# Attention into a feed-forward layer on one core: batch 2's queries and keys by transposed loads instead of TensorE transposes, with a new order of the front

## The chip, the cores and the metric

The kernel runs on one core of a Trainium2 chip. The metric is the device time of one execution in microseconds (us); several executions of the same program are timed and their median is given. One execution is also taken by the hardware profiler; the times inside it are counted from the start of its span.

## The reference

Eight batches of twelve heads, 448 positions, 64 values per head. Attention with a softmax that has one more term in its sum, then a feed-forward layer with a squared relu over all 3,584 tokens. The kernel is given float32 arrays and gives a float32 array.

```python
q, k, v: (8, 12, 448, 64)         # * 0.1
scores = q @ k.T / sqrt(64)
m = max(scores);  e = exp(scores - m)
attn = e / (sum(e) + exp(-m) + 1e-09)
x = (attn @ v).transpose(0, 2, 1, 3).reshape(3584, 768)
h = x @ w_in                      # (768, 2048)
out = (relu(h) ** 2) @ w_out      # (2048, 768)
```

## The kernel before, in words

All matmuls are in float16. For each batch the kernel needs the queries and keys with the 64 values of a head on the partitions (the tile `qk`, two buffers), the values in natural layout (`vn`, two buffers), and then the attention output `xt` as the left side of the first layer.

Queries and keys come to that layout in one of two ways.

- For a batch in `ON_PE` (0, 1 and 2 before), `load_quad` loads a quad (four heads) of q and of k in natural layout into a tile `nn` (line 117, POOL's DMA queue, cast to float16 on the way), `transpose_one` turns it by 14 TensorE transposes for q and 14 for k (line 207), and `transposed_copy` copies the result from PSUM to `qk` (line 215 on ACT, line 217 on VectorE).
- For any other batch, `stage` writes q and k of the batch as float16 to a DRAM buffer (line 155, POOL's queue), `transposed_load` reads it three times with the transposing DMA on SP's queue (line 166): the queries, the keys, and the keys shifted by one row ("planes" 0, 1, 2). Since heads then lie in rows of two positions, the last 64 keys of each head are gathered by `tail_keys`: two POOL copies for each key plane (line 188). The values of such a batch come by four DMAs (line 111), those of a batch in `ON_PE` by one for each quad or one for the batch.

The scores of one chunk of 64 keys of a quad are four matmuls of 64x448 for a batch in `ON_PE` and eight of 64x224 for any other (`quad_scores`, lines 415 and 429); ACT takes the exponential of the chunk (line 254). A score buffer holds one chunk; there are two (`s_psum`). Each quad has seven chunks. Then VectorE adds the chunks (lines 441 to 447), TensorE sums over the partitions (`S`), ACT takes a logarithm (line 463, `Z`) and a negative exponential (line 466, `M`), and VectorE multiplies the values' product by it into `xt` (line 487, `X`).

The first layer of a batch is 16 tiles of six matmuls (`j`, three steps of two each), each followed by a relu (`k`, ACT line 503 or VectorE line 505) and a square (`l`, line 509). The second layer is 56 half tiles of 128 tokens by 384 columns (`o`), 16 blocks of four quarter-array matmuls each, put out by two operations (`O`, `Q`) into one of four output buffers `ot` and stored by DMAs on SP's queue (line 549). First-layer tiles, value products and second-layer tiles share a ring of four PSUM buffers.

The order of all work is written out by hand. `ORDER` is the front: it does the attention of batches 0 to 3, the first layer of batches 0 and 1, and the first 14 half tiles of the second layer. Each word is a step, such as `s48` (scores, exponentials are `e48`), `j11,4,6` or `o1,8,10`; `d` steps are entries of the list `LOADS`. Scores 24 to 44 are batch 1's, 45 to 65 batch 2's, 66 to 86 batch 3's. Behind the front come two runs of `CYCLE` (periods for batches 4 and 6) and a tail of plain first- and second-layer tiles. A step issues its instructions to the engines' queues in this order, and each engine works its own queue off in order, waiting where a semaphore makes it wait. POOL's queue holds its DMA issues and the key copies, SP's queue the transposed loads and the stores. POOL's DMA issues wait, by their semaphores, for the landing of the one issued eight before.

## Time and profile before

| | |
|---|---|
| median of 3 runs | 392.39 us (392.35 to 392.91) |
| profiled execution | 393.06 us |
| its span, first to last instruction | 391.3 us |
| granted TensorE clock | 1.00 |
| busy: TensorE, VectorE, ACT, POOL | 383.2, 251.9, 228.5, 62.2 us |
| POOL's DMA queue (q0) | 22.62 MB, 37.4% of 16 engines' span |
| SP's DMA queue (q1; ACT's first loads are q10) | 21.59 MB, 28.1% |
| first period's first scores start | 135.0 us |

In the profile PE is TensorE's matmuls, DVE is VectorE, L93 is line 93 of the kernel, which is the helper that records nearly every matmul. A row of the timeline gives the start, the length, the engine, the line, the operation with its output and inputs, their shapes and how many instructions were merged into the row. Matmul ends are modelled and overlap, so work on TensorE is best read from one start to the next.

### The profile page before, as it was taken

Reading aid. Unit: us, or ns where it says so; the run is one execution under the profiler, and the core shown is the slowest. Engines: PE = TensorE matmul, PEld = TensorE weight load, DVE = VectorE, ACT = ScalarE, POOL = GpSimd, SP = SyncE. Lnnn points to the kernel's source line nnn. Section 1 sums busy time; section 2 is a strip of 40 time slices with the busy share of each in tenths; the row PEclk is TensorE's granted clock in tenths of the full one; section 3 lists DMA queues with packets and bytes.
Section 4 is the critical chain, followed back from the end, with each engine's and each line's share of the span. In section 5 each row is a group of like instructions: output and inputs, shape, how many; then the busy total and the mean of one; then the engine's idle time right before and its main releaser. Section 6 shows DMA issues by size and latency. Waiting matters only on the chain.

```text
span 391.3 us, 14259 instructions
## 1 busy us (share of the span) xinstructions
PE 383.2 (98%) x6432; PEld 253.7 (65%) x6432; DVE 251.9 (64%) x468; ACT 228.5 (58%) x308; POOL 62.2 (16%) x96
## 2 busy tenths in 40 slices
PE   9789999999999999999999999999999999999997
PEld 5566656565789755667777665667777755556665
DVE  2887995765666766556968757566778788880000
ACT  5999998586689511349988731248988730001221
POOL 8544420025000701300001240310000000000000
PEclk9999999999999999999999999999999999999999
DMA  8999999999939899903129596941112200001132
GB/s 143 203 205 205 202 203 205 182 182 175 215 75 175 158 195 149 160 2 66 44 54 194 145 182 131 151 46 44 52 55 64 64 23 2 0 0 61 62 82 80
DMA packets 75052, 45.34 MB, mean 116 GB/s; under 512 B 47472, under 2 KB 72944, under 8 KB 74992
## 3 DMA queue, kind: packets, MB, share of 16 engines
q0 software_dynamic: 24752, 22.62, 37.4%
q1 hardware_dynamic: 49952, 21.59, 28.1%
q8 instruction: 50, 0.82, 0.9%
q10 hardware_dynamic: 288, 0.23, 0.2%
q14 instruction: 10, 0.08, 0.1%
HBM read 45.69 MB, written 17.93 MB: 163 GB/s over the span
## 4 chain that ended last, share of the span: by engine, by line
PE 86%; ACT 6%; DMA 2%; SPq 2%; DVE 1%; issue 1%; POOL 1%; ACTq 0%; POOLq 0%; DVEq 0%
PE mp L93 77%; PE sp L93 8%; ACT et L254 4%; SPq L166 2%; DMA nn<-in_k_dram 2%; PE mp L207 1%; DMA out_dram<-ot 1%; ACT rcp L372 1%; ACT nn L254 0%; DVE qk L217 0%; ACT rcp L365 0%; ACT ot L575 0%; DVE half L341 0%; ACT rcp L463 0%; DVE half L447 0%
## 5 line engine op out<-in xcount | busy, mean ns | idle before, releaser
L93 PE MATMUL mp<-wout,gs 64*64 64x384 f16 (+2 forms) x2928 | 165.2, 322 | 0.0
L93 PE MATMUL mp<-xt,win 128*64 128x448 f16 (+2 forms) x1188 | 148.3, 347 | 0.1
L93 PEld LDWEIGHTS <-gs 64*64 64x64 f16 (+1 forms) x2928 | 103.1, 106 | 34.5
L93 PEld LDWEIGHTS <-win 128*64 128x64 f16 (+1 forms) x1188 | 83.2, 106 | 63.5 <-issue 4.2
L254 ACT ACTIVATE et<-sp 128x896 f16<-128x896 f32 (+2 forms) x131 | 110.6, 889 | 12.3 <-PE sp L93 11.7
L505 DVE TENSOR_SCALAR rt<-mp 128x448 f16<-128x448 f32 x87 | 54.1, 622 | 17.4 <-PE mp L93 14.5
L509 DVE TENSOR_TENSOR gs<-rt 128x448 f16<-128x448 f16 x128 | 47.8, 390 | 22.1 <-ACT rt L503 20.2
L503 ACT ACTIVATE rt<-mp 128x448 f16<-128x448 f32 x41 | 21.8, 543 | 65.0 <-PE mp L93 55.7
L575 ACT ACTIVATE ot<-mp 128x384 f32<-128x384 f32 (+2 forms) x31 | 14.9, 480 | 71.6 <-PE mp L93 68.8
L93 PE MATMUL sp<-qk 64*64 64x224 f16 (+1 forms) x1056 | 53.7, 274 | 2.1 <-DVE qk L217 0.5
L93 PEld LDWEIGHTS <-qk 64*64 64x64 f16 x1056 | 32.7, 115 | 15.2 <-issue 6.5
L188 POOL COPY flatq<-qk 64x384 f16<-64x384 f16 x20 | 14.8, 739 | 172.7 <-DMA qk<-stage_k 126.0
L254 ACT ACTIVATE nn<-sp 128x896 f16<-128x896 f32 x42 | 37.1, 916 | 4.3 <-PE sp L93 4.2
L487 DVE TENSOR_TENSOR xt<-mp,rcp 128x448 f16<-128x448 f32 x42 | 24.2, 619 | 15.7 <-ACT rcp L466 10.3
L581 DVE SCALAR_TENSOR_TENSOR ot<-mp,ot 128x384 f32<-128x384 f32 x42 | 23.4, 556 | 15.3 <-ACT ot L575 12.4
L93 PEld LDWEIGHTS <-vn 64*64 64x64 f16 x756 | 22.4, 107 | 10.4 <-issue 1.8
L93 PE MATMUL mp<-et,vn 64*64 64x448 f16 (+1 forms) x448 | 24.5, 343 | 0.0
L577 DVE TENSOR_SCALAR ot<-mp 128x384 f32<-128x384 f32 x26 | 14.4, 555 | 14.3 <-PE mp L93 14.2
L463 ACT ACTIVATE rcp<-sp,one_b 128x896 f32<-128x896 f32 x21 | 21.1, 1007 | 2.8 <-PE sp L93 2.7
L466 ACT ACTIVATE rcp<-rcp 128x896 f32<-128x896 f32 x21 | 19.9, 949 | 0.5
L441 DVE TENSOR_TENSOR half<-et 128x1792 f16<-128x1792 f16 x15 | 16.3, 1088 | 4.3 <-ACT et L254 4.2
L443 DVE TENSOR_TENSOR half<-half,et 128x1792 f16<-128x1792 f16 x15 | 16.3, 1086 | 0.3
(59 smaller groups left out, 197.4 us busy)
## 6 DMA issues: line engine op xcount, KB each, us to landing
out_dram<-ot SPq DMA_DIRECT2D x52, 96.0 KB, 2.9
out_dram<-ot SPq DMA_DIRECT2D x19, 192.0 KB, 1.9
win<-in_moe_w_in_dram POOLq DMA_DIRECT2D x8, 384.0 KB, 12.3
wout<-in_moe_w_out_dram POOLq DMA_DIRECT2D x4, 768.0 KB, 14.9
vn<-in_v_dram POOLq DMA_DIRECT2D x10, 288.0 KB, 8.4
stage_q<-in_q_dram POOLq DMA_DIRECT2D x4, 676.0 KB, 13.1
stage_k<-in_k_dram POOLq DMA_DIRECT2D x4, 676.0 KB, 15.9
nn<-in_q_dram POOLq DMA_DIRECT2D x8, 224.0 KB, 8.6
```

Source lines behind the costliest of these rows:

```text
L93: return nc.tensor.matmul(out_, lhsT, rhs, start=start, stop=stop)
L254: nc.scalar.activation(out=out_, in_=in_, func=AF.Exp, scale=scale)
L441: nc.vector.tensor_add(esq[m], a[:, 0:w], a[:, w:2 * w])
L443: nc.vector.tensor_add(esq[m], esq[m], z[:, 0:w])
L463: nc.scalar.activation(out=rcp, in_=zp[:, :, 0:S], func=AF.Ln, bias=one_b)
L466: nc.scalar.activation(out=zqs[m], in_=zqs[m], func=AF.Exp, scale=-1.0)
L487: nc.vector.tensor_mul(xts[b][:, 2 * g + i, :], xqs[m][i][:, 0:S], zqs[m][:, i, :])
L503: nc.scalar.activation(out=rt[:, 0:m], in_=hp[:, 0:m], func=AF.Relu)
L505: nc.vector.tensor_scalar(out=rt[:, 0:m], in0=hp[:, 0:m], scalar1=0.0, scalar2=None, op0=ALU.max)
L509: nc.vector.tensor_mul(gs[:, f0:f0 + per, t0 % RING:t0 % RING + n], r, r)
L575: nc.scalar.activation(out=ot, in_=op[:, 0:w], func=AF.Copy, scale=OUT_SCALE)
L581: nc.vector.scalar_tensor_tensor(out=ot, in0=lo[:, 0:w], scalar=OUT_SCALE, in1=ot, op0=ALU.mult, op1=ALU.add)
```

## The change

Batch 2 leaves `ON_PE`. Its natural loads, transposes and copies go; it is staged, loaded by three transposed loads and gets key copies, like batches 3 and later; its values come by four DMAs. The single steps for the three planes and the two key planes are entries of `LOADS` of their own. The staging of batch 5, which stood in the front (`d31`), is now the step `d7` of the first period. `ORDER` is written anew: batch 0 first, the first layer of batch 0 with the attention of batch 1, then the whole first layer of batch 1 by itself, then the 14 half tiles of the second layer with the attention of batches 2 and 3. In POOL's queue the first two key copies of batch 2 (`d24`) now stand ahead of the second half of `wout` (`d17`, `d18`) and of the staging of batch 3 (`d26`), and the next two (`d25`) ahead of the values of batch 2 (`d20`) and 3 (`d27`). In SP's queue batch 2's three transposed loads (`d22`, `d23`, `d21`) and the first of batch 3 (`d28`) stand ahead of the first stores, the other two of batch 3 (`d30`, `d29`) behind the first and the second pair of stores. The periods and the tail keep their order.

```diff
-    ON_PE = (0, 1, 2)
+    ON_PE = (0, 1)
...
-        x = {(0, 1): (0, 0), (0, 2): (0, 1), (1, 0): (1, 0), (1, 1): (0, 0), (1, 2): (0, 1),
-             (2, 0): (1, 0), (2, 1): (1, 1), (2, 2): (0, 0)}[b, g]
+        x = {(0, 1): (0, 0), (0, 2): (0, 1), (1, 0): (1, 0), (1, 1): (0, 0), (1, 2): (0, 1)}[b, g]
...
-    LOADS = ([lambda b=b, g=g: load_quad(b, g) for b in range(3) for g in range(NQ) if b + g]
+    LOADS = ([lambda b=b, g=g: load_quad(b, g) for b in range(2) for g in range(NQ) if b + g]
              + [lambda b=b, g=g: load_v_quads(b, g, g + 1) for b in range(2) for g in range(NQ)]
-             + [lambda: load_v_quads(2)]
              + [lambda i=i: load_win(i, NW) for i in range(NW)]
-             + [lambda n0=n0, y=y: load_wout(n0, y, 2) for n0 in (0, HALF) for y in range(2)]
-             + [lambda: stage(3), lambda: transposed_loads(3), lambda: tail_keys(3), lambda: load_v_quads(3),
-                lambda: stage(4), lambda: transposed_loads(4), lambda: tail_keys(4), lambda: load_v_quads(4), lambda: stage(5)])
+             + [lambda n0=n0, y=y: load_wout(n0, y, 2) for n0 in (0, HALF) for y in range(2)])
+    for b in (2, 3, 4):
+        LOADS += [lambda b=b: stage(b), lambda b=b: load_v_quads(b)]
+        LOADS += [lambda b=b, i=i: transposed_load(b, i) for i in range(3)]
+        LOADS += [lambda b=b, i=i: tail_keys(b, (i,)) for i in (1, 2)]
...
     ORDER = """
...
+        l8 k2,1 l9 k0,1 l2 j1,0,2 j1,2,4 j13,0,2 j13,2,4 j4,0,2 j4,2,4 j4,4,6 j1,4,6 j14,0,2 j14,2,4 j14,4,6 j13,4,6 k1,1 l0 j15,0,2 k13,0 j15,2,4
+        j15,4,6 l1 j5,0,2 l13 k4,0 d24 d17 d18 d26 k14,1 l4 j5,2,4 j5,4,6 s48 o0,0,2 o0,2,4 k5,1 l14 e48 k15,0 s45 l15 o0,4,6 o0,6,8 o0,8,10 s49 d28
+        o0,10,12 o0,12,14 e45 o0,14,16 s46 e49 e46 s50 O0,0 o1,0,2 Q0 o1,2,4 o1,4,6 o1,6,8 s47 e50 o2,0,2 s55 o2,2,4 o1,8,10 e47 o1,10,12 d25 d20 e55
+        s56 o1,12,14 a3,0 l5 d30 e56 s53 a3,1 o2,4,6 o2,6,8 o1,14,16 e53 s51 O1,1 o2,8,10 s54 o2,10,12 o2,12,14 o2,14,16 e51 j10,0,2 Q1 d29 a3,2
+        j10,2,4 j10,4,6 a3,3 k10,1 j3,0,2 e54 j3,2,4 j3,4,6 O2,0 k3,1 Q2 v3,0 S3 v3,1 v3,2 v3,3 v3,4 Z3 v3,5 v3,6 M3 o5,0,2 s52 e52 o5,2,4 o5,4,6
...
     """
...
-            if t < B and (n != 7 or b > FIRST_PERIOD):
+            if t < B:
```

More of the change, by code (lines that the diff above doesn't have):

```diff
@@ L676 @@
     ORDER = """
-        d0 W8 d8 d1 c1,4,0 c0,0,1 t0,0,0 c1,0,1 t1,0,0 u0,0,0,0 t1,0,4 u1,0,0,0 c0,4,1 u1,0,4,1 t0,0,4 d2 s0 t0,1,0 u0,0,4,1 u0,1,0,0 t1,1,0 u1,1,0,0
-        d10 d9 s1 t0,1,4 e0 t1,1,4 e1 s2 e2 u0,1,4,0 s12 e12 u1,1,4,0 T0,1,0 T0,1,1 U0,1,0,0,4,0 U0,1,1,0,4,0 U0,1,1,4,7,0 U0,1,0,4,7,0 s3 s4 p2 p0 e3
-        b0,0 e4 s6 p1 d18 p3 s5 e6 e5 b0,1 b0,2 T0,2,0 b0,3 y0 T0,2,1 U0,2,0,0,4,0 z0 n0 U0,2,1,0,4,0 b1,0 s8 U0,2,0,4,7,0 U0,2,1,4,7,0 x0 d3 d17 d16
-        b1,1 s9 d15 T1,0,1 e8 e9 U1,0,1,0,7,0 T1,0,0 U1,0,0,0,7,0 b2,0 s11 e11 s10 s13 e10 e13 s14 p8 b2,1 p4 d5 b2,2 p9 s7 e14 p10 b2,3 p11 y2 p5 e7
@@ L681 @@
-        z2 b1,2 p6 s15 b1,3 p7 e15 y1 b3,0 n2 x2 b3,1 z1 s17 e17 b3,2 p12 p13 b3,3 n1 s18 p14 s16 e18 p15 x1 y3 T1,1,0 U1,1,0,0,7,0 e16 b4,0 z3 b4,1
-        s19 e19 i0,6 n3 r0,6,0 s20 e20 s21 i0,7 s22 x3 b4,2 e21 p16 b4,3 e22 b5,0 r0,7,0 p17 p18 p19 d4 b5,1 g0,6 y4 z4 n4 s23 T1,1,1 e23 d13 s27 b5,2
-        x4 i0,4 s28 p20 p21 g0,7 b5,3 e27 p22 p23 y5 U1,1,1,0,7,0 e28 z5 r0,4,0 n5 x5 s26 s29 e26 j20,0,2 j23,0,2 j23,2,4 j20,2,4 j20,4,6 e29 j23,4,6
-        s25 k23,1 s24 g0,4 e25 e24 k20,0 P0 i1,7 j19,0,2 l23 a0,0 s32 e32 a0,1 s36 d6 j19,2,4 e36 j16,0,2 l20 j19,4,6 j17,0,2 s34 s33 k19,1 r1,7,0
@@ L685 @@
-        j17,2,4 j16,2,4 a0,2 l19 e34 j17,4,6 e33 j16,4,6 g1,7 s30 d11 k16,1 s31 e30 k17,0 T2,0,0 T1,2,0 T2,0,1 T1,2,1 l16 s35 e31 U2,0,0,0,7,0
-        U1,2,0,0,7,0 s37 U2,0,1,0,7,1 e35 j18,0,2 j18,2,4 e37 j18,4,6 a0,3 i1,6 d19 S0 U1,2,1,0,7,0 v0,0 a1,0 v0,1 Z0 v0,2 l17 v0,3 v0,4 v0,5 k18,0 d7
-        d12 v0,6 s40 s43 M0 r1,6,0 j27,0,2 a1,1 e43 j22,0,2 j22,2,4 j27,2,4 X0 e40 j27,4,6 l18 j22,4,6 g1,6 a1,2 s39 k27,1 s38 e39 a1,3 d20 T2,2,0 e38
-        k22,0 T2,2,1 T2,1,1 T2,1,0 s41 U2,2,1,0,7,1 U2,2,0,0,7,0 s42 j26,0,2 l27 e41 j21,0,2 j26,2,4 j26,4,6 l22 S1 U2,1,0,0,7,0 e42 U2,1,1,0,7,0 Z1
@@ L689 @@
-        v1,0 v1,1 v1,2 v1,3 v1,4 d23 v1,5 k26,1 v1,6 a2,0 a2,1 a2,2 s44 s47 M1 l26 e44 j21,2,4 d22 j21,4,6 i1,4 X1 a2,3 k21,1 v2,0 v2,1 v2,2 r1,4,0 S2
-        e47 v2,3 Z2 v2,4 v2,5 l21 v2,6 M2 o0,0,4 s46 o0,4,8 d14 s50 e46 e50 o0,8,12 X2 o0,12,16 s51 g1,4 s48 O0,1 Q0 j15,0,2 j0,0,2 j15,2,4 j4,0,2
-        j15,4,6 j4,2,4 j4,4,6 j0,2,4 e51 e48 j0,4,6 s45 k15,1 l15 o2,0,4 s49 e45 e49 o2,4,8 s52 d21 o2,8,12 a3,0 e52 o2,12,16 k4,1 k0,0 s53 a3,1 s55
-        d24 j10,0,2 O2,1 j1,0,2 Q2 j10,2,4 j1,2,4 j10,4,6 l0 j14,0,2 l4 j1,4,6 j11,0,2 e55 k10,0 j14,2,4 a3,2 j11,2,4 k1,1 j8,0,2 l10 j14,4,6 j11,4,6
@@ L693 @@
-        k11,1 j9,0,2 a3,3 j8,2,4 j9,2,4 e53 l1 j8,4,6 j9,4,6 k14,0 s57 l14 e57 l11 S3 Z3 v3,0 d25 v3,1 v3,2 v3,3 k9,0 k8,0 v3,4 v3,5 v3,6 M3 o1,0,4
-        s54 o1,4,8 X3 s56 o1,8,12 o1,12,16 e54 a4,0 O1,0 s63 e56 o5,0,4 s58 o5,4,8 Q1 e63 a4,1 a4,2 s65 e58 a4,3 o5,8,12 e65 s60 o5,12,16 e60 O5,1 s59
-        v4,0 v4,1 Q5 v4,2 v4,3 l9 S4 v4,4 e59 Z4 M4 v4,5 v4,6 o4,0,4 o4,4,8 s61 o4,8,12 o4,12,16 e61 s64 O4,1 X4 s62 j2,0,2 l8 Q4 j2,2,4 j2,4,6 j7,0,2
-        k2,1 j5,0,2 e62 j7,2,4 j7,4,6 k7,0 l7 d27 j12,0,2 j6,0,2 e64 a5,0 j12,2,4 j5,2,4 l2 j5,4,6 k5,1 j6,2,4 j6,4,6 j12,4,6 a5,1 j13,0,2 j13,2,4
@@ L697 @@
-        j13,4,6 l5 a5,2 j3,0,2 j3,2,4 j3,4,6 k12,0 a5,3 s69 l12 k6,1 o3,0,4 l6 k13,1 k3,1 l3 S5 l13 o3,4,8 o3,8,12 o3,12,16 O3,0 Q3 e69 s70 Z5 s71 d26
-        M5 v5,0 v5,1 v5,2 v5,3 e70 e71 v5,4 v5,5 v5,6 o9,0,2 o9,2,4 X5 o9,4,6 o9,6,8 s66 o9,8,10 s68 o9,10,12 o9,12,14 o9,14,16 e66 O9,0 o6,0,2 e68
-        s67 s72 o6,2,4 o6,4,6 o6,6,8 e67 o6,8,10 Q9 a6,0 a6,1 e72 a6,2 s73 o8,0,2 o6,10,12 o6,12,14 o8,2,4 o6,14,16 s75 e73 O6,0 o8,4,6 o8,6,8 e75 s78
-        Q6 o8,8,10 o8,10,12 a6,3 e78 o8,12,14 s79 o8,14,16 s77 v6,0 v6,1 v6,2 v6,3 e79 e77 v6,4 S6 v6,5 v6,6 Z6 M6 s74 O8,0 Q8 o7,0,2 o7,2,4 e74 X6
@@ L701 @@
-        o7,4,6 s76 e76 a7,0 o7,6,8 o7,8,10 o7,10,12 o7,12,14 a7,1 o7,14,16 s82 d28 o10,0,2 O7,1 o10,2,4 o10,4,6 Q7 o10,6,8 s80 a7,2 e82 o10,8,10
-        o10,10,12 o10,12,14 o10,14,16 e80 s85 s83 o11,0,2 o11,2,4 e85 o11,4,6 o11,6,8 d31 O10,1 Q10 e83 s81 a7,3 d29 o11,8,10 o11,10,12 o11,12,14 e81
-        o11,14,16 O11,1 Q11 s84 o12,0,2 s86 o12,2,4 o12,4,6 e84 e86 o12,6,8 o12,8,10 a8,0 o12,10,12 o12,12,14 o12,14,16 S7 a8,1 O12,0 o13,0,4 o13,4,8
-        d30 o13,8,12 Z7 Q12 a8,2 o13,12,16 v7,0 v7,1 v7,2 v7,3 O13,1 v7,4 a8,3 v7,5 v7,6 M7 S8 Q13 v8,0 v8,1 Z8 v8,2 v8,3 M8 v8,4 v8,5 X7 v8,6 X8
+                 d0 c1,4,0 c0,0,1 c1,0,1 W8 c0,4,1 t0,0,0 t1,0,0 u0,0,0,0 u1,0,0,0 t1,0,4 t0,0,4 u1,0,4,0 u0,0,4,1 s0 t0,1,0 t1,1,0 s1 u0,1,0,0 e0
@@ new lines @@
+        t0,1,4 u1,1,0,0 e1 s2 t1,1,4 u0,1,4,0 d5 s12 T0,1,0 u1,1,4,0 U0,1,0,0,4,0 e2 T0,1,1 e12 U0,1,1,0,4,0 U0,1,0,4,7,0 d1 s3 d2 e3 s4 p2 b0,0 p0 d6
+        b0,1 e4 p3 s5 b0,2 e5 p1 s15 T0,2,0 d7 d14 d13 b0,3 e15 y0 U0,1,1,4,7,0 s7 U0,2,0,0,4,0 T0,2,1 d3 U0,2,0,4,7,0 U0,2,1,0,4,0 z0 d12 e7 s6 d4 e6
+        s9 U0,2,1,4,7,0 s8 n0 e9 d11 b1,0 T1,0,0 s11 e8 T1,0,1 b1,1 b1,2 U1,0,0,0,7,0 e11 s10 x0 d8 b2,0 e10 s13 U1,0,1,0,7,0 s14 b1,3 b2,1 b2,2 p4
+        e13 p8 e14 p5 p6 b2,3 p7 y1 p9 b3,0 z1 p10 p11 s19 y2 z2 n2 b3,1 e19 x2 s16 n1 b3,2 s18 p12 p13 b3,3 p14 e16 p15 y3 x1 e18 s17 e17 i0,7 b4,0
@@ new lines @@
+        z3 s21 s20 n3 e21 b4,1 b4,2 x3 b4,3 i0,6 r0,7,0 s22 e20 e22 p16 p17 p18 p19 y4 z4 b5,0 r0,6,0 s23 n4 i0,4 b5,1 s27 x4 b5,2 e23 b5,3 s24 p20
+        p21 g0,7 p22 p23 e27 y5 s26 g0,6 T1,1,1 e24 z5 r0,4,0 n5 U1,1,1,0,7,0 s28 e26 T1,1,0 x5 j20,0,2 U1,1,0,0,7,0 j20,2,4 j20,4,6 k20,0 s25 e28 P0
+        e25 s29 g0,4 l20 i1,6 e29 r1,6,0 s36 s32 g1,6 T1,2,0 T1,2,1 e36 U1,2,0,0,7,0 a0,0 e32 s34 i1,7 a0,1 s33 e34 s30 j23,0,2 U1,2,1,0,7,0 r1,7,1
+        j16,0,2 j23,2,4 j23,4,6 j16,2,4 a0,2 e33 e30 g1,7 s31 a0,3 d19 s35 j16,4,6 e31 e35 j22,0,2 k16,0 j22,2,4 k23,0 j22,4,6 l23 s37 v0,0 S0 v0,1
@@ new lines @@
+        v0,2 v0,3 v0,4 v0,5 v0,6 l16 k22,0 e37 s43 j21,0,2 Z0 j18,0,2 j21,2,4 j18,2,4 e43 s40 M0 s38 e40 e38 l22 j21,4,6 a1,0 a1,1 X0 j18,4,6 k18,0
+        j17,0,2 a1,2 l18 j17,2,4 k21,1 s41 e41 s39 d9 d10 j17,4,6 i1,4 d22 e39 s44 d16 a1,3 d23 l21 s42 j26,0,2 r1,4,1 j26,2,4 e42 k17,0 a2,0 l17 g1,4
+        a2,1 j19,0,2 j26,4,6 j19,2,4 e44 j19,4,6 a2,2 S1 v1,0 v1,1 k26,1 k19,0 v1,2 v1,3 d15 v1,4 v1,5 a2,3 l19 v2,0 v1,6 v2,1 Z1 S2 v2,2 M1 v2,3 Z2
+        l26 v2,4 v2,5 X1 v2,6 M2 j27,0,2 j27,2,4 j27,4,6 k27,1 j11,0,2 X2 l27 j11,2,4 j7,0,2 j7,2,4 j11,4,6 j6,0,2 j7,4,6 j6,2,4 d21 k7,1 j6,4,6 k11,0
@@ new lines @@
+        j8,0,2 j8,2,4 j8,4,6 j12,0,2 j12,2,4 j12,4,6 l7 k6,1 j9,0,2 j2,0,2 j9,2,4 l6 j9,4,6 l11 k12,1 l12 k8,0 j2,2,4 j0,0,2 k9,0 j2,4,6 j0,2,4 j0,4,6
+        l8 k2,1 l9 k0,1 l2 j1,0,2 j1,2,4 j13,0,2 j13,2,4 j4,0,2 j4,2,4 j4,4,6 j1,4,6 j14,0,2 j14,2,4 j14,4,6 j13,4,6 k1,1 l0 j15,0,2 k13,0 j15,2,4
+        j15,4,6 l1 j5,0,2 l13 k4,0 d24 d17 d18 d26 k14,1 l4 j5,2,4 j5,4,6 s48 o0,0,2 o0,2,4 k5,1 l14 e48 k15,0 s45 l15 o0,4,6 o0,6,8 o0,8,10 s49 d28
+        o0,10,12 o0,12,14 e45 o0,14,16 s46 e49 e46 s50 O0,0 o1,0,2 Q0 o1,2,4 o1,4,6 o1,6,8 s47 e50 o2,0,2 s55 o2,2,4 o1,8,10 e47 o1,10,12 d25 d20 e55
@@ new lines @@
+        s56 o1,12,14 a3,0 l5 d30 e56 s53 a3,1 o2,4,6 o2,6,8 o1,14,16 e53 s51 O1,1 o2,8,10 s54 o2,10,12 o2,12,14 o2,14,16 e51 j10,0,2 Q1 d29 a3,2
+        j10,2,4 j10,4,6 a3,3 k10,1 j3,0,2 e54 j3,2,4 j3,4,6 O2,0 k3,1 Q2 v3,0 S3 v3,1 v3,2 v3,3 v3,4 Z3 v3,5 v3,6 M3 o5,0,2 s52 e52 o5,2,4 o5,4,6
+        o5,6,8 s57 o5,8,10 l3 X3 a4,0 l10 e57 d27 s58 o5,10,12 o5,12,14 o5,14,16 s65 o6,0,2 O5,0 e58 d32 Q5 a4,1 s63 e65 d31 o6,2,4 o6,4,6 o6,6,8 s59
+        e63 o6,8,10 e59 s60 e60 o6,10,12 o6,12,14 o6,14,16 o3,0,2 s62 O6,0 s61 o3,2,4 o3,4,6 o3,6,8 o3,8,10 e62 e61 s64 a4,2 o3,10,12 e64 Q6 a4,3 s69
@@ new lines @@
+        a5,0 o4,0,2 o4,2,4 a5,1 o3,12,14 s67 o3,14,16 e69 o4,4,6 O3,0 S4 o4,6,8 a5,2 o4,8,10 e67 Q3 o4,10,12 o4,12,14 o4,14,16 a5,3 O4,0 Q4 v4,0 v4,1
+        v4,2 d33 Z4 S5 M4 v4,3 v4,4 v4,5 v4,6 X4 v5,0 v5,1 v5,2 v5,3 v5,4 v5,5 v5,6 s68 Z5 M5 e68 o7,0,2 d37 s71 o7,2,4 o7,4,6 e71 o7,6,8 s75 e75 X5
+        o8,0,2 s70 d35 o8,2,4 o7,8,10 o8,4,6 o7,10,12 s66 o7,12,14 e70 e66 o7,14,16 s74 o8,6,8 o8,8,10 O7,0 s72 Q7 e74 o8,10,12 o8,12,14 o8,14,16
+        o9,0,2 s73 O8,0 o9,2,4 e72 Q8 s76 o9,4,6 o9,6,8 o10,0,2 e73 s79 o9,8,10 e76 s78 e79 o10,2,4 o9,10,12 e78 s77 e77 a6,0 a7,0 a6,1 o10,4,6
@@ new lines @@
+        o9,12,14 s85 o10,6,8 a7,1 o9,14,16 o10,8,10 s83 o10,10,12 e85 s84 O9,1 e83 o10,12,14 Q9 o10,14,16 e84 d39 o12,0,2 a6,2 O10,0 o12,2,4 o12,4,6
+        Q10 o12,6,8 a7,2 a6,3 o12,8,10 s81 s80 o12,10,12 e81 e80 o12,12,14 o12,14,16 o11,0,2 s82 d34 d36 o11,2,4 o11,4,6 o11,6,8 O12,0 S6 Q12 e82
+        o11,8,10 Z6 o11,10,12 s86 o11,12,14 a7,3 o11,14,16 a8,0 v6,0 v6,1 O11,1 v6,2 v6,3 v6,4 a8,1 v6,5 Q11 M6 v6,6 S7 d38 v7,0 v7,1 X6 v7,2 v7,3
+        v7,4 v7,5 Z7 v7,6 e86 a8,2 M7 a8,3 X7 o13,0,2 o13,2,4 o13,4,6 o13,6,8 o13,8,10 o13,10,12 o13,12,14 o13,14,16 O13,0 S8 v8,0 v8,1 v8,2 v8,3 v8,4
@@ L705 @@
+        v8,5 Q13 v8,6 Z8 M8 X8
     """
```

## The prediction

> **What bounds the kernel now.** I read the page first, then the busy time by stretches, then TensorE's timeline at the steps that the change touches, then the transfers.

> ```profile
> PE 383.2 (98%) x6432; PEld 253.7 (65%) x6432; DVE 251.9 (64%) x468; ACT 228.5 (58%) x308; POOL 62.2 (16%) x96
> DMA  8999999999939899903129596941112200001132
> GB/s 143 203 205 205 202 203 205 182 182 175 215 75 175 158 195 149 160 2 66 44 54 194 145 182 131 151 46 44 52 55 64 64 23 2 0 0 61 62 82 80
> ```

> TensorE is busy all the way, so matmul work that goes is time that goes, unless a new wait fills it. One slice is 9.8 us: up to slice 8 (78 us) the transfers run flat out at about 0.204 MB per us.

> ```profile
> 10.00:30.00 20.00, 16.48 (x422) 12.50 (x420) 17.47 (x40) 19.63 (x31) 9.61 (x14) 1.00 1.25 204
> 30.00:60.00 30.00, 29.81 (x410) 17.70 (x404) 26.02 (x49) 28.03 (x39) 10.56 (x14) 1.00 1.24 204
> 60.00:110.00 50.00, 49.77 (x842) 31.23 (x844) 30.75 (x57) 36.65 (x50) 7.81 (x12) 1.00 1.09 188
> 135.00:315.00 180.00, 180.00 (x3614) 123.79 (x3610) 123.56 (x223) 110.89 (x142) 19.74 (x32) 1.00 0.59 100
> ```

> The columns after the length are PE, PEld, DVE, ACT, POOL, the granted clock, the DMA share and GB/s. To 60 us ACT (19.63 of 20, 28.03 of 30) sets the pace, VectorE just behind it; then TensorE alone does, at full clock. The change lies ahead of 135 us; the two periods and the tail stay.

> **TensorE's work.** Start to start in the timeline: two matmuls of the first layer take 0.38 us, eight of the second 0.33, four of values or one score chunk 0.19; a change between whole-array and quarter-array matmuls costs 0.10 more.

> ```profile
> 40.18 0.57 PE L93 MATMUL sp<-qk 64*64 64x448 f16 x8
> 40.68 1.69 PE L93 MATMUL mp<-xt,win 128*128 128x448 f16 x8
> 42.30 0.57 PE L93 MATMUL sp<-qk 64*64 64x448 f16 x8
> 42.80 1.75 PE L207 MATMUL mp<-ident,nn 128*64 128x128 f16 x56
> 44.48 0.57 PE L93 MATMUL sp<-qk 64*64 64x448 f16 x8
> ...
> 103.73 0.58 PE L93 MATMUL sp<-qk 64*64 64x224 f16 x16
> 104.11 1.52 PE L93 MATMUL mp<-nn,vn 64*64 64x448 f16 x28
> ```

> Removed: batch 2's six blocks of 14 transposes. Four blocks go from 42.80 to 44.48, 0.42 each: 6 x 0.42 = 2.5 us. Batch 2's 21 score chunks become eight 64x224 matmuls instead of four 64x448: two chunks take 0.38 (103.73 to 104.11) in the new form, 0.50 in the old one beside first-layer tiles and 0.38 inside second-layer tiles, so nothing is lost. Set up over the whole order with these prices, TensorE's work ahead of the first period is 123.8 us before and 121.6 after: 2.2 us less. In the trace that period's first scores start at 135.0, so 11.2 us ahead of it is waiting: 9.0 by 24.3 us (15.3 us of work done by then), 10.0 at the start of the second layer (61.65 us, 51.6 us of work done), and small waits behind.

> **The stage that ACT paces.** ACT loses two copies of 930 ns and gets one first copy less; VectorE loses four of 618 ns. What has to end before batch 1's first layer is the reciprocal of its third quad, which now ends at 63.1 (62.15 and 0.95). With the page's busy times (0.87 an exponential, 1.0 a logarithm, 0.95 a reciprocal, 0.53 a relu) the new order puts 53.9 us of ACT work ahead of it against 58.1, but 0.5 of what went lay ahead of the first exponential, which waits for scores anyway. So it ends at about 63.1 - 4.2 + 0.5 = 59.4, its product (two of 0.62) at 60.6. TensorE has 51.0 us of work before the matmul that needs it: at 10.0 of waiting it comes at 61.0. Both meet, so the waiting stays 10.0 and ACT's saving buys nothing. The 14 us of first-layer tiles behind it need neither exponentials nor new loads. TensorE then reaches batch 2's first scores with 65.6 us of work behind it (75.6 us), its first values with 78.0 (88.0), batch 3's first scores with 88.5 (98.5). From 75.6 on ACT has 51.5 us of work under TensorE's 56: close, but summed between any two uses of a score buffer, ACT's durations exceed TensorE's by 0.1 us at most.

> **The transfers** decide the rest. Removed: six natural loads (0.23 MB each) and batch 2's single v load; added: staging of batch 2 (1.38 MB, first written to DRAM), three transposed loads (0.69 MB each), four key copies, v by four issues (2.65 us of POOL for four). Staging of batch 5 moves behind the front, and batch 5 is first needed some 54 us into the period (189.4 less 135.0): nothing. Batch 2's stores go out in fewer pieces: nothing. The finer second-layer steps: nothing.

> ```profile
> 67.23 9.40 SPq L166 DMA_TRANSPOSE qk<-stage_q  x1
> 76.69 6.09 SPq L166 DMA_TRANSPOSE qk<-stage_k  x2
> ...
> 117.55 4.21 SPq L166 DMA_TRANSPOSE qk<-stage_q  x1
> ```

> The first of these landed 11.9 us after its issue, beside wout; alone, 117.55 took 6.5. The transfers by queue, 142 to 146 us, a transposed load (q1) beside staging (q0):

> ```profile
> DMA packets 413, 0.69 MB, mean 173 GB/s; under 512 B 221, under 2 KB 221, under 8 KB 413
> q0 software_dynamic: 208, 0.64, 97.5%
> q1 hardware_dynamic: 205, 0.05, 15.5%
> ```

> Packet for packet the queues share evenly, but staging's packets are twelve times as large, so a transposed load beside staging crawls at 0.013 MB per us; beside v (250 to 258 us) q1 gets 0.53 MB and q0 0.69 in 8 us; alone (78 to 84) 0.24 MB per us. [...]

> Now the new order. The third v load lands at 17.9 us. From there win (3.15 MB), four natural loads (0.92), a v (0.23) and batch 2's staging (1.38) take 5.68 / 0.204 = 28 us: staged at 46. The first transposed load runs beside two wout loads, 12 to 15 us: landed 58 to 61. Only then do POOL's key copies (1.3 us for two) let it issue the other two wouts and batch 3's staging. Staging issued at 88.04 to an idle queue landed after 6.4 us, 3.4 of them moving; so the first new bytes come some 4 us after the landing. In that lull the other two transposed loads need 1.38 / 0.24 = 5.8 us, more if wout catches them: landed 64 to 70, needed at 75.6. Wait: zero. Wout's second half is in by 74 (needed at 79), batch 3's staging by 80.5. Batch 2's v then shares with batch 3's q plane: 8 us, landed about 88.5 (84 to 91), needed at 88.0: 0.5 us. On SP this q plane stands ahead of the first stores, and those ahead of batch 3's key planes; stores have four buffers, whose first is needed again at 98, so SP's wait costs TensorE only through the planes. The q plane lands at about 90.5, each key plane 4 to 6 us behind the one before it with two stores between: the last at 100.5 (98.5 to 102.5), needed at 98.5 plus the 0.5. So TensorE waits about 1.5 us there, 12.0 in all, and I add 0.3 for small waits behind it: 121.6 + 12.3 = 133.9 against 135.0, 1.1 us less. The profiled execution of 393.06 (span 391.3) would be 392.0; it lies 0.67 above the median of 392.39, so the median is 391.3.

> **Rivals.** (1) Everything lands in time: then 121.6 + 10.6 = 132.2, 2.8 less: 389.6. For it: the lull, and 0.24 MB per us alone. Against it: the chain of three planes on one queue behind staging. [...] (2) Slower: batch 2's last plane (q) is still on its way when batch 3's staging starts at 74. It then crawls until staging ends at 80.5, lands at about 82, and TensorE stands at batch 2's first scores for 6 us: 121.6 + 16.4 + 0.3 = 138.3, 3.3 more: 395.7. It decides if that plane has over 0.1 MB left at 74; I count 4 us of margin on a chain whose first load is uncertain by 3. (3) The same chain for batch 3, 3 us later than I put it (the row of 135.72 held SP 15.96 us): 1.5 to 3 more than before, 394 to 395.5. (4) Batch 4's planes wait for a later staging and hold the stores behind them until the output buffers run out near 125 us: 1 us on top of the forecast, 392.4. (5) The change not doing what it says: the new order of instructions has the transposes out, so no chance.

> **Numbers.** Forecast 0.42, its own range 389.8 to 393.3 (the last plane from 99 to 102.5); rival 1 0.20; rival 2 0.18; rival 3 0.16; rival 4 0.04. A measurement of this kernel tells 0.2%, 0.8 us. The forecast is faster by more than that in 0.26, within it in 0.15, slower in 0.01. With rival 1 faster has 0.46; same has 0.17 with half of rival 4; slower 0.37. The range goes from 389.4 (rival 1) to 395.6 (rival 3 and most of rival 2).

> **What would show it.** In the profile after: no L207 matmuls of batch 2; TensorE at batch 2's first scores at 75 to 76 without a wait; a wait on a transposed load at batch 3's first scores, near 99, and perhaps a short one on v near 88. Wrong if the wait stands at batch 2's first scores, if neither is there, or if the periods (180 us) change.

## The result and the profile after

| | before | after |
|---|---|---|
| median of 6 runs on one chip | 392.76 us (392.35 to 394.53) | 397.07 us (395.93 to 399.12) |
| profiled execution | 393.06 us | 395.93 us |
| its span | 391.3 us | 394.1 us |
| start of the first period's first-layer tile `j14` | 135.7 us | 138.5 us |

The ratio is 1.0106, with a 95% interval from 1.0075 to 1.0138: slower by 1.1%. I had forecast 391.3, with 389.4 to 395.6 as the range; the time lies outside it and on the other side of no change.

The two profiled executions differ by 2.8 us of span, and all of it is there when the first period starts. Set up with the prediction's prices, TensorE's work up to `j14` is 124.2 us before and 121.9 us after, so the time in which TensorE waited is 11.5 us before (135.7 less 124.2) and 16.6 us after: 2.3 us of work saved, 5.1 us of waiting added. The periods keep their 180 us.

First the profile's page and the busy time by stretches, as the prediction showed them for the kernel before. The columns after the length are PE, PEld, DVE, ACT, POOL, the granted clock, the DMA share and GB/s.

```profile
PE 382.7 (97%) x6432; PEld 257.2 (65%) x6432; DVE 254.9 (65%) x470; ACT 225.4 (57%) x300; POOL 62.3 (16%) x99
DMA  8999999999979999921118897931122200001132
GB/s 144 204 205 210 205 175 217 210 160 181 174 159 189 192 180 181 207 30 52 56 43 164 172 171 141 169 36 44 43 63 63 63 22 0 2 0 57 64 82 80
```

```profile
60.00:110.00 50.00, 46.96 (x845) 34.88 (x846) 30.18 (x55) 31.91 (x42) 14.82 (x22) 1.00 1.22 188
```

TensorE was busy 49.77 of these 50 us before; now it is 46.96. The stretch from 76 to 98 us, the same answer for the kernel before and then for the kernel after, shows what changed there:

```profile
76.00:98.00 22.00, 21.77 (x347) 12.85 (x345) 14.23 (x26) 16.43 (x21) 7.81 (x12) 1.00 0.92 179
```

```profile
76.00:98.00 22.00, 19.62 (x470) 15.68 (x465) 12.14 (x20) 17.33 (x22) 1.34 (x3) 1.00 1.33 177
```

The same GB/s, but the DMA engines are occupied by 1.33 instead of 0.92 of their number (over 1: the packets' times add up to more than the stretch), and TensorE runs 470 short matmuls instead of 347, in less busy time. What TensorE waited for, in the list of waits of the kernel after (total, times, longest):

```profile
PE sp L93 <- ACT et L254: 2.9, 5, 1.2
PE mp L93 <- issue: 2.7, 2, 2.2
...
PE sp L93 <- DMA qk<-stage_k: 0.7, 1, 0.7
PE sp L93 <- issue: 0.4, 2, 0.2
...
PE mp L93 <- DVE ot L581: 0.2, 1, 0.2
```

The first row lies ahead of 31 us, where ACT sets the pace, and TensorE's busy time from 10 to 30 us is as it was (16.46 and 16.48). The wait for a transposed load that I forecast is there, 0.7 us, at step `s69`, batch 3's first scores. The largest new row behind 31 us has "issue" as its releaser: TensorE stood and no semaphore held it. In the timeline of TensorE the two long ones are these:

```profile
93.70 0.42 PE L93 MATMUL mp<-wout,gs 64*64 64x384 f16 x4
96.31 0.35 PE L93 MATMUL mp<-wout,gs 64*64 64x384 f16 x3 [2.18 <-issue]
...
122.16 0.68 PE L93 MATMUL mp<-wout,gs 64*64 64x384 f16 x11 [0.53 <-issue]
```

Both lie in the middle of a second-layer output, between two matmuls of one accumulation. The profile page's queue list names a queue that I had passed over:

```profile
q8 instruction: 50, 0.82, 0.9%
```

0.82 MB in 50 packets, for a program of 12,864 matmuls and weight loads on TensorE: by division 64 bytes for each, and 16,384 bytes a packet (the trace has this size for all 50), so by this estimate one packet holds 128 matmuls with their loads. I call these a page of code. I read it as TensorE's own code, which e1 and e3 below bear out; the page counts its packets over the same 16 DMA engines as the data's. The two stops lie at matmuls 1373 and 2013 of the trace, 640 apart, which is five packets exactly. Around the first one the transfers by queue are, from 89.1 to 93.3 us and then from 93.3 to 95.1:

```profile
q0 software_dynamic: 1060, 0.38, 74.9%
q1 hardware_dynamic: 1285, 0.47, 62.6%
```

```profile
q1 hardware_dynamic: 672, 0.17, 182.6%
q8 instruction: 1, 0.02, 5.7%
```

For 4.2 us the engines serve v (q0) and transposed loads (q1) and no code; then the one packet comes. Read so, packet by packet, with the matmuls counted in steps of 128:

| page begun | next page's packet starts | it has landed | next page begins | idle there |
|---|---|---|---|---|
| 77.06 | 79.36 | 80.34 | 81.72 | 0 |
| 81.72 | 86.27 | 87.53 | 89.02 | 0.20 |
| 89.02 | 93.40 | 95.04 | 96.31 | 2.18 |
| 111.78 | 114.47 | 115.40 | 116.79 | 0.13 |
| 116.79 | 119.62 | 120.61 | 122.16 | 0.53 |
| 126.85 | 130.54 | 131.50 | 132.91 | 0.10 |

In these six rows the packet of the next page starts while the present one runs, 2.3 to 4.6 us behind its beginning; it takes 0.9 to 1.6 us to land, and TensorE goes on 1.3 to 1.6 us behind its landing. Inside the second layer a page lasts 4.6 to 4.7 us here. So by an estimate (4.7 less 1.0 of moving and 1.3 from landing to use) a packet that starts more than some 2.4 us behind the beginning of its page stops TensorE: in the table 2.30 us cost nothing and 2.69 cost 0.13, in e9 below 2.46 us stopped nothing, in e11 2.57 cost 0.06. Five packets of the table did stop it, for 3.1 us in all.

The profile of the kernel before had one such row, which I did not follow up: its list of waits holds 0.5 us of it, at 22.11 us, 1.30 behind the landing of a code packet at 20.81.

```profile
PE sp L93 <- issue: 0.5, 1, 0.5
```

The long stop of 2.18 us is not on the chain of work that ended last, though. That chain, and SP's own timeline, lead into batch 3's first scores like this:

```profile
97.26 5.46 DMA qk<-stage_k
102.76 0.40 PE sp L93 x7
```

```profile
86.06 9.88 SPq L166 DMA_TRANSPOSE qk<-stage_k  x1
96.03 1.18 SPq L549 DMA_DIRECT2D out_dram<-ot  x2
97.26 3.37 SPq L166 DMA_TRANSPOSE qk<-stage_k  x1
```

The first key plane held SP until 95.94 us, so the second could hardly go out earlier, and it landed at 102.72. Had the code come in time, TensorE would have stood at `s69` for it instead, by an estimate some 3.5 us in place of 0.7: without the stop it reached this step at 98.9 to 99.6 us in e2, e5, e7, e10 and e11 below. What sat beside the planes is one more transfer, which my prediction had left out of this stretch: batch 3's v. POOL's queue ran ahead of TensorE and issued it right behind batch 2's v; it landed between 89.97 and 95.93 us.

```profile
70.26 0.65 POOL L111 DMA_DIRECT2D vn<-in_v_dram  x1 [2.04 <-DMA wout<-in_moe_w_out_dram]
...
81.65 0.64 POOL L111 DMA_DIRECT2D vn<-in_v_dram  x1 [3.91 <-DMA stage_k<-in_k_dram]
```

### The profile page after: what moved, and what is told of

Same layout as the page of the kernel before. It is cut to its first block, busy times and chain, and to the rows that moved or that the text cites. A ratio compares the mean times of both kernels' runs of the same rounds, so it can differ in the third digit from the quotient of the medians.

```text
span 394.1 us, 14269 instructions
## 1 busy us (share of the span) xinstructions
PE 382.7 (97%) x6432; PEld 257.2 (65%) x6432; DVE 254.9 (65%) x470; ACT 225.4 (57%) x300; POOL 62.3 (16%) x99
## 4 chain that ended last, share of the span: by engine, by line
PE 89%; ACT 4%; DVE 3%; DMA 2%; issue 1%; SPq 0%; DVEq 0%; ACTq 0%
PE mp L93 78%; PE sp L93 9%; ACT et L254 2%; PE xp L93 2%; DMA qk<-stage_k 1%; DMA out_dram<-ot 1%; PE mp L207 1%; ACT rcp L372 1%; PE mp L234 0%; DVE half L343 0%; DVE half L341 0%; DVE xt L487 0%; DVE ot L581 0%; SPq L549 0%; DVE qk L217 0%
## 5 line engine op out<-in xcount | busy, mean ns | idle before, releaser
L93 PE MATMUL mp<-wout,gs 64*64 64x384 f16 (+2 forms) x2928 | 168.8, 322 | 2.7 <-issue 2.7
L93 PE MATMUL mp<-xt,win 128*64 128x448 f16 (+2 forms) x1188 | 148.3, 347 | 0.0
L93 PEld LDWEIGHTS <-gs 64*64 64x64 f16 (+1 forms) x2928 | 107.8, 106 | 33.6 <-issue 3.4
L93 PEld LDWEIGHTS <-win 128*64 128x64 f16 (+1 forms) x1188 | 83.2, 106 | 63.4 <-issue 4.3
L509 DVE TENSOR_TENSOR gs<-rt 128x448 f16<-128x448 f16 x128 | 49.6, 406 | 23.6 <-ACT rt L503 21.7
L93 PE MATMUL sp<-qk 64*64 64x224 f16 (+1 forms) x1116 | 56.8, 267 | 4.5 <-ACT et L254 2.9
L575 ACT ACTIVATE ot<-mp 128x384 f32<-128x384 f32 (+2 forms) x26 | 12.4, 478 | 70.0 <-PE mp L93 68.8
L93 PEld LDWEIGHTS <-qk 64*64 64x64 f16 x1116 | 37.2, 116 | 17.8 <-issue 9.4
L188 POOL COPY flatq<-qk 64x384 f16<-64x384 f16 x24 | 16.7, 695 | 168.2 <-DMA qk<-stage_k 122.4
L577 DVE TENSOR_SCALAR ot<-mp 128x384 f32<-128x384 f32 x31 | 17.2, 555 | 23.2 <-PE mp L93 23.0
L487 DVE TENSOR_TENSOR xt<-mp,rcp 128x448 f16<-128x448 f32 x42 | 24.2, 619 | 10.1 <-ACT rcp L466 6.8
L93 PEld LDWEIGHTS <-vn 64*64 64x64 f16 x756 | 23.5, 107 | 9.8 <-issue 1.6
L93 PE MATMUL mp<-et,vn 64*64 64x448 f16 (+1 forms) x448 | 25.4, 344 | 0.3 <-DVE ot L581 0.2
L111 POOL DMA_DIRECT2D vn<-in_v_dram x24 | 15.6, 664 | 11.5 <-DMA wout<-in_moe_w_out_dram 5.0
```

Of the source, the lines that this page charges most:

```text
L93: return nc.tensor.matmul(out_, lhsT, rhs, start=start, stop=stop)
L188: nc.gpsimd.tensor_copy(km[rows_].rearrange("p h (x o) -> p h x o", o=2)[:, :, :, odd], src[:, :, S // 2 - 32:S // 2])
L487: nc.vector.tensor_mul(xts[b][:, 2 * g + i, :], xqs[m][i][:, 0:S], zqs[m][:, i, :])
L509: nc.vector.tensor_mul(gs[:, f0:f0 + per, t0 % RING:t0 % RING + n], r, r)
L577: nc.vector.tensor_scalar(out=ot, in0=op[:, 0:w], scalar1=OUT_SCALE, scalar2=None, op0=ALU.mult)
```

## The experiments

Theory P: TensorE's code comes late behind the data. Theory W/B: the loss is the chain that I forecast, planes and stores on SP. Theory Q or O: the idle belongs to the work or the order, whatever is transferred. "Profiled" below is one execution; medians are of 4 to 10 runs (e1 and e4 ran once), and the kernel before, run beside them, had medians from 392.29 to 392.83.

**Page edges moved** (e1_shift): 64 small matmuls at the very start.

```diff
         for _ in range(n):
             mm(aside()[:, 0], idle[:, 0:128], idle, start=True, stop=True)
+        for _ in range(64):
+            mm(aside()[0:64, 0, 0:64], idle[0:64, 0:64], idle[0:64, 0:64], start=True, stop=True)
```

> The changed kernel with 64 small 64x64 matmuls of 64 columns at its very start, so that every later matmul is number n + 64 and each page of TensorE's code (128 matmuls with their loads) ends 64 matmuls earlier in the order; nothing else is moved. Theory P (TensorE stands because the next page of its code has not arrived): the idle of 2.18 us with no releaser leaves its place in the middle of o6 (matmul 1373 of the changed kernel) and the idle without a releaser is found at matmuls that are a multiple of 128 away from 1309 of the old count (in o5,6,8 near 91.7, near s73, near s78), each 1.3 to 1.6 us behind the end of the code packet. Theory Q (the idle belongs to the work at that step: a buffer, a throttle of the clock): 2 us still at o6, number 1437 now. The time may be 3 us longer by the start alone.

Its timeline of TensorE, and the clock (the number before the DMA share) around the stop:

```profile
91.25 0.38 PE L93 MATMUL sp<-qk,flatq 64*64 64x224 f16 x7 [1.95 <-issue]
```

```profile
90.00:92.00 2.00, 0.75 (x25) 0.75 (x28) 1.02 (x2) 0.32 (x1) 0.00 (x0) 0.98 0.98 135
92.00:94.00 2.00, 2.00 (x31) 1.51 (x22) 0.62 (x1) 0.59 (x1) 0.00 (x0) 0.50 1.31 187
94.00:96.00 2.00, 2.00 (x10) 0.88 (x8) 1.11 (x2) 0.00 (x0) 0.00 (x0) 0.67 1.28 275
```

o6 runs through. The stops (1.95 and 1.22 us) are at matmuls 1181 and 1565 of the old count: 128 before 1309 and 256 behind it. Theory P, and the edge of the page, not the step, is the place. The run, 400.34 us, shows a second price: behind the stop the granted clock is 0.50 for 3.4 us.

**Batch 3's v later** (e2_v3_late).

```diff
-        ... e57 d27 s58 ... d32 Q5 a4,1 s63 e65 d31 o6,2,4 ...
+        ... e57 s58 ... d32 Q5 a4,1 s63 e65 d31 d27 o6,2,4 ...
```

> The changed kernel with batch 3's v loads issued by POOL behind both key copies of batch 3 (after some 103 us) instead of ahead of them (90 to 96). Theory P: with 0.69 MB of v out of the way the code page that started 4.4 us late at 93.4 starts within 2.5 us, its 2.18 us of idle falls under 0.6; batch 3's planes land 3 to 4 us earlier, so the wait of 0.66 us at s69 goes; the pages of 103 to 122 may lose up to 0.5 us each. Sum: 1.5 to 3 us less than the changed kernel. Theory W (the loss is the planes' chain as forecast, and the idle without a releaser is something of its own): 0.7 to 0.9 us less, and the 2.18 us stay.

Profiled 395.15, median 396.44. The packet of the page of 88.73 us starts 2.63 us behind its beginning, where it was 4.38, and the 2.18 us are gone; so is the wait at `s69`: batch 3's planes landed at 89.0, 93.4 and 97.5 us instead of 93.8, 97.9 and 102.7. Of "issue" 1.0 us is left. The edit takes away both the late code and the late planes ahead of `s69`, so it does not tell what each is worth in time. And the sum was not kept: a new row stands in the list of waits.

```profile
PE mp L93 <- ACT ot L575: 2.1, 1, 2.1
```

The copy of an output out of PSUM waits for an output buffer, whose store waits on SP behind batch 4's planes: the mechanism of my rival 4, in this kernel.

**Half the instructions** (e3_half_rows).

```diff
-                for y in (0, 64):
-                    for x, o in ((0, op), (64, lo)):
-                        mm(o[y:y + 64, 0:w], g[x:x + 64, y:y + 64], wout[x:x + 64, fb, n0:n0 + w],
-                           start=(fb == 0), stop=(fb == NFFB - 1))
+                for x, o in ((0, op), (64, lo)):
+                    mm(o[:, 0:w], g[x:x + 64, :], wout[x:x + 64, fb, n0:n0 + w],
+                       start=(fb == 0), stop=(fb == NFFB - 1))
```

> The changed kernel with every block of the second layer done by two matmuls of 64 rows by 128 columns instead of four of 64 by 64: the same products, half the instructions, so a page of code lasts twice as long inside the second layer (9 to 10 us instead of 4.7). Theory P: every code page is in before it is needed and the idle without a releaser (3.1 us in five places of the front) is gone: 3 us less, if a change between 64x64 and 64x128 matmuls costs nothing. If it costs 0.10 us as between whole-array and quarter-array ones, the 86 changes in the front and 156 in the periods cost up to 24 us, which hides the gain in the time but not in the list of idles. Theory Q: the idles of 2.2 and 0.5 us at o6 and o10 stay.

418.67 us: the changes of form cost what was feared. The code queue moves 40 packets for 5,088 matmuls, again 128 to a packet. The gain is in the waits: pages last 8 to 10 us here, every packet from 70 us on lands 5.5 us or more ahead of its use, and TensorE has no stop over 0.15 us from 40 to 160 us, of any cause. The kernel is also 22 us slower than its neighbour, so its transfers have more time; alone it would not prove P.

**Traffic alone, on the kernel before** (e4_before_traffic).

```diff
+    def extra(i):
+        for n, t in (("q", q), ("k", k)):
+            st = nc.dram_tensor(f"extra_{n}{i}", (HSD,), FP16, kind="Internal").ap()
+            nc.gpsimd.dma_start(out=st.rearrange("(r w) -> r w", w=1024), in_=..., max_dma_last_dim=8192)
...
-        ... d31 ...
+        ... d31 D0 D1 ...
```

> The kernel before, with two more stagings of 1.38 MB each from DRAM to DRAM queued on POOL right behind that of batch 5; nobody reads them. They keep the DMA engines in use from 100 to about 124 us, where TensorE runs the second layer and a page of code lasts 4.7 us. Theory P: the code pages of that stretch start 2 to 4 us late instead of 0.1 to 2.3, and TensorE stands without a releaser for 0.3 to 3 us in all between 105 and 130, in a kernel that has none of the change. Theory Q: no idle without a releaser there. Either way the first period's planes may land some us later (they have until 155).

397.15 us in the one run, span 395.3. Its waits and its timeline:

```profile
PE sp L93 <- issue: 3.4, 3, 1.6
PE mp L93 <- issue: 1.3, 1, 1.3
```

```profile
115.72 0.48 PE L93 MATMUL mp<-wout,gs 64*64 64x384 f16 x5 [1.34 <-issue]
...
121.91 0.35 PE L93 MATMUL sp<-qk 64*64 64x224 f16 x5 [1.02 <-issue]
...
128.38 0.35 PE L93 MATMUL sp<-qk 64*64 64x224 f16 x5 [1.59 <-issue]
```

Data that nobody reads costs 4 us of TensorE's time in a kernel without the change: three neighbouring pages, whose packets start 3.8 to 4.0 us late. Plain staging does it as well as transposed loads do. With e1 this settles that code comes late behind data and stops TensorE. It does not say how much of the changed kernel's loss that is.

**Output buffers** (e5_v3_late_osb6): e2 with `osb` of 6 buffers instead of 4.

> The run with batch 3's v late (e2_v3_late), with six output buffers instead of four and no other edit. In that run TensorE stood 0.25 + 0.48 + 2.46 + 0.41 = 3.6 us around batch 3's values (126.5 to 131.6) for a copy into an output buffer whose store was held on SP behind batch 4's planes. Theory B (output buffers run out, since SP holds the stores): those 3.6 us go to under 0.5, and the time falls by about 3 us against that run. Theory P alone (only late code costs time; the values would wait for something else): no change.

Profiled 393.10, median 394.74: the waits at batch 3's values are gone. 1.3 us come back at the first period's first scores, which now reach batch 4's last plane before it has landed; the net is 2.1 in the profiled executions. Over the kernel before, run beside each of the two, the medians go from 3.6 to 2.4 us more.

**Batch 4's transfers earlier and together, then apart** (e6_stage4_first, e7_last_plane_apart).

```diff
-  ... d31 d27 ... d33 ... d37 ... d35 ... Q8 ... d34 d36 ...
+  ... d31 d33 d27 ... d37 ... d35 d36 ... Q8 ... d34 ...        (e6)
+  ... d31 d33 d27 ... d37 ... d35 ... Q8 d36 ... d34 ...        (e7)
```

> The run with batch 3's v late, with batch 4's staging issued ahead of that v on POOL, and SP issuing batch 4's three planes one behind the other where the first stood. Staging lands near 109 instead of 115, the planes are in by 120 instead of 136, and the stores held behind them go out from 119 on. Theory B: the 3.6 us at batch 3's values fall under 0.8. Theory P: v and planes now meet between 108 and 118, so a code page there may come 0.3 to 1 us later than its use. Sum: 2 to 3.5 us less than the run with v late.

> As the run before, but batch 4's last plane behind the stores of output 8, so that SP holds the stores twice for 4 us instead of once for 10. Theory B: the buffers never run out, the waits at batch 3's values are under 0.5 us, and the time is the same as the run before or up to 0.5 us less.

e6 went the other way: 398.24 median. SP held the stores from 109.97 to 123.40 us behind three planes in a row, and the code came late four times. Its list of waits:

```profile
PE sp L93 <- issue: 2.9, 3, 1.6
PE mp L93 <- DVE ot L581: 1.7, 2, 1.4
PE mp L93 <- issue: 1.3, 1, 1.3
```

e7, the same transfers with the last plane apart, ran at 392.58 profiled and has no wait for outputs; 1.2 us of late code stay. Its other three runs were 394.41 to 396.62, two of them at a mean clock of 0.999 and 1.000: median 395.51. What they lost is not shown.

**One part undone** (e8_order_alone): batch 2 back on TensorE, in the new order.

```diff
-    ON_PE = (0, 1)
+    ON_PE = (0, 1, 2)
...
+             (2, 0): (1, 0), (2, 1): (1, 1), (2, 2): (0, 0)}[b, g]
...
+    LOADS[19] = lambda: [load_quad(2, g) for g in range(NQ)]
...
-  ... X2 l27 ... k7,1 ... k11,0 ... (with d21 to d25)
+  ... X2 l27 T2,0,0 ... k7,1 U2,0,0,0,7,0 T2,0,1 ... k11,0 U2,0,1,0,7,1 T2,1,0 ... (without them)
```

> The changed kernel's order with one part of the change undone: batch 2 comes by natural loads again and its six blocks of 14 transposes stand between first-layer tiles of batch 1 (62 to 74 us), so TensorE has about 2.5 us more to do than in the changed kernel; its staging, three transposed loads and key copies are gone, and all transfers behind them move forward by some 10 us. Theory P (late code, because batch 2's transfers push those of batch 3 into the second layer): the idle without a releaser between 80 and 135 falls from 3.1 to under 0.5 us, the wait at s69 goes, and the kernel is level with the one before within 1.5 us (391.5 to 393.5). Rival O (the new order itself puts too many short matmuls in one stretch, whatever is transferred): the idles stay, 398 to 400.

Profiled 394.80, median 395.23. "issue" is down to one row:

```profile
PE mp L93 <- issue: 0.3, 1, 0.3
```

Waiting up to `j14` is 11.9 us, level with the kernel before (11.5) and 4.7 under the changed one, and batch 3's last plane lands at 96.2 us; so the stops and the late planes come from batch 2's transfers, which push those of batch 3 into the second layer, and not from the order (rival O falls). The pages between 80 and 100 us are somewhat longer here too, since a chunk of batch 2's scores is four matmuls; but up to 138 us no packet starts more than 2.75 us late, where it was 4.5. The time was still 1.3 us over its expected end. In the trace a block of transposes takes 0.52 us (63.20 to 63.71) and the two first-layer matmuls behind it 0.48 instead of 0.38, so six blocks cost some 3.6 us, not 2.5; and a wait of 0.6 us for a relu is new.

**Transfers spread** (e9_less_at_once, e10_q_plane_late, e11_v_behind_stage), all with six output buffers and batch 4's v (`d34`) behind its last key copy (`d38`):

```diff
   e9:   ... d31 d33 ... d37 d39 d27 ... Q8 d36 ... d38 d34 ...
   e10:  e9, and  s49 d28 ... Q0  ->  s49 ... Q0 d28
   e11:  e10, and  d31 d33 ... d37 d39 d27  ->  d31 d33 d27 ... d37 (d39 where it was)
```

> The changed kernel with its transfers from 85 us on spread: batch 3's v behind batch 4's first key copy, batch 4's staging ahead of it, batch 4's last plane behind the stores of output 8, batch 4's v behind its last key copy, and six output buffers. Theories P and B together: no wait at batch 3's first scores and none at its values; idle without a releaser 0.2 to 0.8 us in all. In the profiled run 390 to 392, which is 4 to 5 us under the changed kernel. If code is late wherever anything is transferred, 1 to 2 us of it stay, and other executions lie higher by as much.

> The run before with batch 3's q plane issued by SP behind the stores of output 0 (about 85 us) instead of ahead of them, so that it no longer meets batch 2's v. Theory P: the page of code of 81.7 us starts 1 to 2.5 us late instead of 4.5 and its 0.2 us of idle goes. Price: batch 3's planes land 2 to 3 us later, so 0 to 1.5 us of wait at batch 3's first scores. Together within 0.5 us of the run before.

> The run before (e10_q_plane_late) with batch 3's v issued right behind batch 4's staging instead of behind batch 4's first key copy, where TensorE stood 1.36 us for it (127.4 and 129.6). Theory P: that wait goes, v now meets the staging, and the pages of 103 to 114 lose 0.3 to 1 us instead of 0.07 + 0.41. Sum: 0.3 to 1 us less than that run; 391.5 to 392.5 in an execution at full clock.

e9 did not get there: 396.44 median. Late code fell to 0.47 us, but v was now too late itself, and the clock fell behind the stop. From its timeline and its busy time by stretches:

```profile
129.33 0.95 PE L93 MATMUL mp<-et,vn 64*64 64x448 f16 x16 [2.71 <-DMA vn<-in_v_dram]
```

```profile
131.00:132.00 1.00, 1.00 (x20) 0.46 (x13) 1.00 (x3) 0.57 (x1) 0.21 (x1) 0.50 1.01 197
132.00:133.00 1.00, 1.00 (x16) 0.51 (x12) 0.82 (x1) 1.00 (x2) 0.94 (x2) 0.50 0.55 118
133.00:134.00 1.00, 1.00 (x16) 0.61 (x12) 0.62 (x1) 1.00 (x2) 1.00 (x3) 0.52 0.46 103
```

e10: 394.00 median (392.7 to 399.6), no idle at the page of 88.50, v still 1.4 us late. e11: profiled 391.80, median 392.53 of 10 runs (390.88 to 393.86), ratio to the kernel before 0.9992 (0.9968 to 1.0016). Its first period's first scores start at 133.7 us (135.0 in the kernel before, 137.8 in the changed one). Of the waits that the change added two rows are left:

```profile
PE mp L93 <- issue: 0.5, 1, 0.5
PE sp L93 <- issue: 0.4, 1, 0.4
```

Four steps of loads moved in order, one v behind the key copies and two more buffers take the change from 1.1% slower to level. A version faster than both was not found.

**First-layer tiles spread** (e12_tiles_spread): e11 with `j13 j4 j14 j15 j5` set between the outputs of 82 to 100 us, `o6` behind `v5`.

> The run beside it (e11_v_behind_stage) with five first-layer tiles of batch 1 (5.75 us, 12 instructions each) taken from ahead of batch 2's scores and set between the second-layer outputs of 82 to 100 us, outputs of tokens 384 to 511 moved behind batch 2's values. Work and transfers are the same; the pages of code between 80 and 100 now last 6 to 7 us instead of 4.7. Theory P: no idle without a releaser before 100 us in any case; batch 2's scores come at 70 us, 2 us behind their planes. The time is level with the run beside it or up to 1 us less in the profiled execution, and spreads less between executions. Rival (exponentials now come too close together, ACT paces it): 1 to 3 us of waits for a score buffer between 70 and 85.

Late code before 100 us is 0.01 us, as theory P has it, and the median is 395.41, 2.9 over e11. The rival's waits came, but later than it said: batch 2's scores wait 1.2 us for score buffers at 94 and 97 us, and second-layer outputs wait 1.0 for copies out of PSUM at 112. The rest of the 2.9 is open: in the profiled execution the clock had already fallen to 0.50 at 11.2 to 14.6 us, so its span of 395.8 says nothing.

## Why the prediction was wrong

- **TensorE's work**: right. The 84 transposes are gone, the sum up to the first period's scores has 2.2 us less, and batch 2's scores came at 75.7 (75.6 forecast).
- **The ACT-paced stage**: right. The third reciprocal ended at 59.7 (59.4), and the waiting at batch 2's scores was 10.1 (75.7 less 65.6 of work; 10.0 forecast).
- **The transfers up to batch 3's staging and batch 2's v**: right. Batch 2's staging 46.05 (46), its first plane 59.9 (58 to 61), the others 63.8 and 68.0 (64 to 70), wout 73.6 (74), batch 3's staging 81.4 (80.5), v 86.9 (88.5, so no wait where I had 0.5).
- **Batch 3's planes**: this step failed. The prediction has the q plane share the engines with batch 2's v alone and does not count batch 3's v. With it the q plane landed at 93.8 (90.5) and the last key plane at 102.7 (100.5, at most 102.5); with that v out of the way (e2) they landed at 89.0 and 97.5. TensorE went on at 102.8 where I had 100.5. That is 2.3 of the 3.9 us by which the first period's first scores came late (137.8 for 133.9), and it is what rival 3 described, for a reason that it did not name.
- **The wait at batch 3's scores**: 0.9 us from start to start (0.66 of it idle) instead of 1.5. That it is so near is luck: two stops for code had already taken 2.4 us of the same time. Since the plane ended last, those stops should have cost nothing on top of it; this is read from the trace, for no run takes away one of the two without the other.
- **"0.3 for small waits behind it"**: this term failed too. Behind `s69` it held three stops for code (0.76 us of idle; from start to start they took 0.39, 0.85 and 0.45 where 0.11, 0.11 and 0.18 are usual, so 0.17 more for each restart and 1.3 in all) and 0.4 for output buffers at 132 us, near where rival 4 had put them. With the 2.3 this makes 4.0, less the 0.3 that I had: 3.7 of the 3.9 us.
- **The rivals**: none of the five named TensorE's code. The range reached 395.6 through late planes; the profiled execution, at 395.93, lies just beyond it, and the median another 1.1 us.

Where the steps went wrong: my list of what moves from 76 to 96 us lacked batch 3's v, which POOL issued at 70 to 82 us although TensorE first reads it at 130. And I took the DMA engines to serve data only, and asked of each transfer whether its own reader would wait. The trace of before had the code queue in its list of queues and a wait without a releaser, with nothing else to explain it.

One more term had no place in my sum: a slow stretch behind a stop. In e1 (1.95 us idle) and e9 (2.71) the clock was then 0.50 for 3.4 us, by an estimate some 1.7 us of time (half of 3.4). The changed kernel's profiled execution (2.18 us idle) and e2's (2.12) kept their clock. The traces' records of the clock suggest a reason, which no run tests. In e1 and e9 the changes of the clock lie at multiples of 3.413 us from one another (e1: 13.40, 91.91, 95.33 us, 23 and 1 of them; e9: 4.25, 130.54, 133.96, 37 and 1). The 3.41 us that ended where the clock fell held 1.95 us of idle in e1 and 2.2 in e9. In the changed kernel the record of the full clock begins at 6.48 us and lasts 389.12, 114 of these steps; an edge counted on from there, at 95.23 (26 steps), cuts the stop into 1.10 and 1.08, and in e2 the fullest stretch held 1.7. How much idle it takes is not known from this: in e12 the clock fell behind a stretch with 1.6 us of idle in several waits.

Of the changed kernel's six runs four had a mean clock of 0.995 or 0.996, which in e1 and e9 is one slow stretch. That the median lies 1.1 us above the profiled run fits; it is argued, for only one of the six has a trace. It is not all of it either: one run at a clock of 1.00 took 397.15, and three of seven runs of the kernel before, beside e1, had 0.991 or 0.996.
